# Batch 0's first 256 tokens alone through VectorE and ScalarE, with q and k loaded by kinds and layer one in tiles of four blocks

## The chip, the cores and the metric

The kernel runs on one core of a Trainium2 chip. The metric is the device time of one execution in microseconds (us); lower is better. PE is TensorE (DVE is VectorE, ACT is ScalarE, POOL is GpSimd, SP is SyncE), and "SPq" and "POOLq" are queues from which DMAs are issued.

## The reference, cut to what matters

Eight batches of eight heads, 576 tokens, head dimension 64. Heads 0 to 3 attend to the last 32 tokens ("plain"), heads 4 to 7 to every fourth of the last 128 tokens ("class": four residue classes of tokens, each a plain window of its own). The heads of a token are joined to a row of 512 values, and two dense layers follow.

```
scores = 0.125 * q @ k.T
plain   (heads 0-3): 0 <= rel < 32
dilated (heads 4-7): 0 <= rel < 128 and rel % 4 == 0
attn = softmax(where(mask, scores, -1e9));  x = attn @ v      # 4608 x 512
h = x @ w_in        # 512 x 2048
out = (h * sigmoid(h)) @ w_out     # 2048 x 512
```

## The kernel before, in words

The order of the work is written out by hand: under `tc.manual_schedule()` every engine executes its instructions in the order in which the Python code issues them, and the framework adds the semaphore waits. A batch passes through these steps (z = 0 is the plain kind, z = 1 the class kind):

- **Loads** (`load_qk`, `load_qk0`, `load_v`, `load_w_in`, `load_w_out`), all issued by POOL, with a cast from f32 to f16. POOL has eight semaphores for its DMAs and uses them in turn, so an issue waits until the DMA issued eight places earlier has landed. Two copies of `v` shifted by 32 tokens are made by small copies (`shift_plain`, `shift_class`, `shift_over`), for batch 0 partly on DVE and partly as DMAs from SP.
- **transpose** (L274; `transpose0` for batch 0, L301 class and L314 plain): PE turns q and k, DVE or ACT copy them out of PSUM into `kT`, `qT` (plain) and `kC`, `qC` (class).
- **scores** (L324 plain, L336 class): 32 x 64 products. For batch 0 the mask is laid into PSUM first by a product (`masks0`, L380) and the scores are added to it.
- **softmax**: the negative row maximum (`maxima0` L403, or L464), then either one subtraction on DVE (`shift0` L421) and one wide exponential on ACT (`exps` L487), or one narrow exponential for each slot with the maximum as bias and the sum read beside it (`exps` L496). `normal` then takes the sum (L505, only for the wide form), adds epsilon (L509), takes the reciprocal (L510) and multiplies (L512, the tile `pn`).
- **turn** and **turned**: PE transposes `pn` (L521) and DVE or ACT copy it out (L529, the tile `ptT`). **values0** (L580, L618) or **values** (L554, L618): the products with `v`; **finish0** (L593), **finish** (L631) and **last_finish** copy them into `xT`.
- **Layer one** (`layer1` L644; `layer1_part` L664 for batch 0): products with `w_in`, then silu on ACT into `gT` (L652, L671). **Layer two** (`layer2_first` L681 for batch 0, `layer2` L707): products with `w_out`, a copy (L691) and a store (L692).

Later batches run their attention inside the dense layers of the batch before: `plan_of(b)` keeps a list of steps, and `plan(s)` emits what is due at step s between two blocks of products. From batch 1 on the change moves only the transposes of batch 1 (in the steps of batch 0).

Batch 0 has nothing to hide behind. It is cut into part 0 (tokens 0 to 255) and part 1 (256 to 575). Before, the prologue runs part 0 and part 1 interleaved through the engines: the scores of part 1 follow those of part 0 on PE, and its maxima, shifts and exponentials stand on DVE and ACT between the steps of part 0. `keep_busy` (L841) fills waits of PE with products of the identity matrix. Then `layer1_part(f, part)` makes two of the 16 blocks of 128 features at a time, all 16 blocks for part 0 and then all for part 1; a tile `h` of two PSUM banks holds two blocks, and the pool `big` has two such tiles. In the steps -16 to -2 between the blocks of part 0 stand what is left of part 1's attention (`normal` and the steps after it), `clear_v(1)`, and the loads of v of batch 1, of w_out's last two quarters and of batch 2's q and k. The transposes of batch 1's class kind are at step 2, its scores at step 8, the transposes of its plain kind at step 17 and their scores at step 20 (steps 16 to 31 are in `layer2_first`, one for every four products).

The order of POOL's loads before: q and k of part 0 (two DMAs of all eight heads), q and k of part 1, v's first class group and plain heads, w_in's first quarter, v's second group and short rest, w_in's other quarters, batch 1's q and k (eight DMAs), w_out's first two quarters, batch 1's v.

Of the kernel before, what the change touches and what calls it, by code (L numbers as in the profile page):

```python
# [8 lines left out]
F16 = mybir.dt.float16  # L9
# [19 lines left out]
def kernel(  # L29
# [44 lines left out]
    ident_b = cpool.tile([P, P], BF16, name="ident_b")  # L74
    mask_b = cpool.tile([P, 2, 2, KB], BF16, name="mask_b")
    band_b = cpool.tile([P, KB], BF16, name="band_b")
# [18 lines left out]
    def load_qk(b):  # L95

        for which in (0, 1):
            t = nat.tile([P, H * 8, D], F16, tag=f"n{which}", name=f"n{which}_{b}")
            u0, u1 = 2 * URS[0], 2 * (URS[0] + URS[1])
            qk[b, 0, which] = t[:, 0:u0].rearrange("p (h u) d -> p h u d", h=2)  # L100
            qk[b, 1, which] = t[:, u0:u1].rearrange("p (h u) d -> p h u d", h=2)
        for z in (1, 0) if b == 1 else (0, 1):
# [8 lines left out]
    def load_qk0(part):  # L111

        t0, n = ((0, PA), (SA, PB))[part]
        qk0[part] = [None, None]
        for which, src in ((1, k), (0, q)):
            t = nat.tile([P, H * 8, D], F16, tag=f"n{which}", name=f"n{which}_0{part}")
            t = qk0[part][which] = t[:, 0 : H * UR].rearrange("p (h u) d -> p h u d", h=H)
            nc.gpsimd.dma_start(
                out=t[0:n],
                in_=src[0, :, t0 : t0 + n * UR].rearrange("h (p u) d -> p h (u d)", u=UR),  # L120
            )
# [77 lines left out]
    band = cpool.tile([P, KB], F32, name="band")  # L199
    nc.vector.memset(band[0:W], 0.0)  # L200
    clear_v(0, nc.vector)
    load_qk0(0)
# [10 lines left out]
    load_qk0(1)  # L213
    load_v(0, ("first", "plain"))
    shift_over(0, nc.sync.dma_start)
    shift_plain(0, nc.sync.dma_start, 4, NM)
    load_w_in(0, 1)
    load_v(0, ("second", "short"))
# [9 lines left out]
    for n in (1, 2, 3):  # L228
        nc.vector.tensor_copy(band[n * W : n * W + W], band[0:W])

    def lay_mask(m):
        n = 2 * m.shape[2]
        nc.vector.tensor_copy(
            m.rearrange("p a t c -> p (a t) c"), band[:, None, :].broadcast_to([P, n, KB])
        )
        nc.vector.memset(m[0:W, 0, 0, 0:W], NEG)
        nc.vector.memset(m[:, 1, 0, 0:W], NEG)

    lay_mask(mask_b)
    nc.vector.tensor_copy(ident_b, ident)  # L240
    nc.vector.tensor_copy(band_b, band)
# [699 lines left out]
```

## Time and profile before

| | us |
|---|---|
| median of 3 runs | 324.84 (324.49 to 325.32) |
| the profiled execution | 324.54 |
| its span, first to last instruction | 322.8 |
| outside the span | 1.7 |
| PE busy in the span | 311.8 |
| ACT, DVE, POOL busy | 214.7, 180.1, 83.2 |
| mean granted PE clock | 0.999 |

"Busy" counts the time in which at least one instruction of the engine is in flight. In a timeline line stand the start, the length of the whole merged group, engine, line, operation, output from input with sizes, the number of instructions, and in brackets how long the engine sat idle before it and for whom. In the chain of waits a line is one link of the chain that ended last. In a table of windows the number ahead of a bracket is the busy time of that engine in that stretch.

### The profile page before, as it was taken

The numbers are of one execution on the slowest core, as the hardware profiler recorded it, in microseconds if no ns is written. First come the engines' busy times: TensorE is split into PE (matmuls) and PEld (weight loads), VectorE is DVE, ScalarE is ACT, GpSimd is POOL, SyncE is SP. The second block draws the span as 40 slices with busy tenths as digits, with TensorE's granted clock in tenths as the row PEclk, the third lists the DMA queues.
The fourth block names the chain that finished last, engine by engine and source line by source line (L and its number), as shares of the span: only waits on it lengthen the run. The fifth ranks groups of instructions, "written<-read, shape, count | busy, mean of one in ns | idle before, by whom it ended". The sixth has DMA issues, their size and how long they took to land.

```text
span 322.8 us, 11769 instructions
## 1 busy us (share of the span) xinstructions
PE 311.8 (97%) x5151; PEld 202.0 (63%) x5151; DVE 180.1 (56%) x379; ACT 214.7 (67%) x700; POOL 83.2 (26%) x140
## 2 busy tenths in 40 slices
PE   5899999999999999999999999999999999999995
PEld 2667754677446775577645776567745776467544
DVE  5896679736597556663665446662576423620011
ACT  1776657657999569965896458975799357736300
POOL 8545537418404430335005700050000000000000
PEclk9999999999999999999999999999999999999999
DMA  8999999938924990298119840191011100110021
GB/s 108 187 212 198 184 230 204 227 99 124 184 86 83 129 146 36 73 163 133 26 68 140 170 80 2 67 174 37 5 52 49 65 4 0 68 67 0 2 97 67
DMA packets 45668, 32.63 MB, mean 101 GB/s; under 512 B 21264, under 2 KB 40336, under 8 KB 45616
## 3 DMA queue, kind: packets, MB, share of 16 engines
q0 software_dynamic: 39520, 21.73, 49.1%
q1 hardware_dynamic: 5952, 10.08, 8.5%
q8 instruction: 40, 0.66, 0.8%
q14 instruction: 12, 0.10, 0.1%
q10 hardware_dynamic: 144, 0.07, 0.1%
HBM read 37.75 MB, written 9.44 MB: 146 GB/s over the span
## 4 chain that ended last, share of the span: by engine, by line
PE 87%; DVE 6%; ACT 3%; issue 1%; POOL 1%; DMA 1%; POOLq 0%
PE h L644 35%; PE o L707 33%; PE h L664 4%; PE t L274 3%; PE x L554 3%; PE pt L521 2%; PE o L681 2%; PE s L336 2%; PE s L324 1%; DVE pn L512 1%; DVE ms L448 1%; ACT pe L496 1%; DVE nm L464 1%; PE x L580 1%; DVE ob L691 1%
## 5 line engine op out<-in xcount | busy, mean ns | idle before, releaser
L707 PE MATMUL o<-w_out,gT 128*128 128x512 f16 (+1 forms) x528 | 115.6, 373 | 0.0
L644 PE MATMUL h<-xT,w_in 128*128 128x288 f16 x896 | 115.4, 286 | 0.0
L652 ACT ACTIVATE gT<-h 128x576 f16<-128x576 f32 x112 | 72.8, 650 | 61.9 <-PE h L644 61.2
L644 PEld LDWEIGHTS <-w_in 128*128 128x128 f16 x896 | 85.7, 98 | 23.0 <-DVE xT L631 0.3
L496 ACT ACTIVATE pe<-ms,nm 128x64 f32<-128x64 f32 x246 | 81.6, 333 | 3.3 <-DVE nm L464 3.2
L707 PEld LDWEIGHTS <-gT 128*128 128x128 f16 x528 | 50.1, 98 | 53.0
L691 DVE COPY ob<-o 128x512 f32<-128x512 f32 (+1 forms) x36 | 24.6, 682 | 52.5 <-PE o L707 52.1
L496 ACT ACTIVATION_READ_ACCUMULATOR pe<-ms,nm 128x1 f32 x246 | 46.0, 187 | 0.0
L448 DVE SCALAR_TENSOR_TENSOR ms<-s,mask 128x512 f32<-128x512 f32 x28 | 19.2, 686 | 41.4 <-PE s L336 25.0
L127 POOL DMA_DIRECT2D vw<-in_v_dram x16 | 10.1, 640 | 76.9 <-PE x L554 75.5
L512 DVE TENSOR_TENSOR pn<-pe,r 128x640 f16<-128x640 f32 (+2 forms) x32 | 25.3, 792 | 1.1
L631 DVE CAST xT<-x 128x512 f16<-128x512 f32 x27 | 17.4, 686 | 12.0 <-PE xs L618 12.0
L464 DVE TENSOR_REDUCE nm<-ms 128x10 f32<-128x640 f32 (+1 forms) x28 | 22.0, 787 | 1.0
L106 POOL DMA_DIRECT2D n<-in_k_dram x28 | 16.5, 602 | 14.6 <-PE t L274 5.2
L106 POOL DMA_DIRECT2D n<-in_q_dram x28 | 16.4, 605 | 10.0 <-DMA w_out<-in_moe_w_out_dram 5.4
L664 PE MATMUL h<-xT,w_in 128*128 128x256 f16 (+1 forms) x128 | 17.9, 295 | 0.5 <-ACT gT L671 0.5
L529 DVE COPY ptT<-pt 128x640 f16<-128x640 f16 (+1 forms) x27 | 11.7, 468 | 8.0 <-PE pt L521 8.0
L664 PEld LDWEIGHTS <-w_in 128*128 128x128 f16 x128 | 12.5, 101 | 4.7 <-issue 1.2
L681 PE MATMUL o<-w_out,gT 128*128 128x512 f16 x64 | 15.1, 380 | 0.0
L671 ACT ACTIVATE gT<-h 128x512 f16<-128x512 f32 (+1 forms) x16 | 10.3, 650 | 7.1 <-PE h L664 6.9
L521 PE MATMUL pt<-ident,pn 128*128 128x128 f16 x152 | 12.4, 224 | 1.4 <-DVE pn L512 1.2
L521 PEld LDWEIGHTS <-pn 128*128 128x128 f16 x152 | 10.1, 99 | 4.7 <-DVE pn L512 1.5
(102 smaller groups left out, 267.6 us busy)
## 6 DMA issues: line engine op xcount, KB each, us to landing
out_dram<-ob SPq DMA_DIRECT2D x35, 256.0 KB, 2.1
n<-in_k_dram POOLq DMA_DIRECT2D x28, 144.0 KB, 5.4
n<-in_q_dram POOLq DMA_DIRECT2D x28, 144.0 KB, 5.5
vw<-in_v_dram POOLq DMA_DIRECT2D x8, 288.0 KB, 6.7
vw<-in_v_dram POOLq DMA_DIRECT2D x16, 128.0 KB, 4.8
w_in<-in_moe_w_in_dram POOLq DMA_DIRECT2D x4, 512.0 KB, 11.6
w_out<-in_moe_w_out_dram POOLq DMA_DIRECT2D x4, 512.0 KB, 10.6
vw<-vw POOLq DMA_DIRECT2D x12, 128.0 KB, 2.8
```

Of the source, the lines that this page charges most:

```text
L106: nc.gpsimd.dma_start(out=qk[b, z, which][i * HF : i * HF + UPS[z]].rearrange("p h u d -> p h (u d)"), in_=src[b, h : h + 2].rearrange("h ...
L448: nc.vector.scalar_tensor_tensor(out=ms[:, 0:8].rearrange("p (n t) c -> p n (t c)", n=2), in0=s[hi].rearrange("p n t c -> p n (t c)"), sca ...
L464: nc.vector.tensor_reduce(out=nm[:, 0:w], in_=ms[:, 0:w], axis=AX.X, op=ALU.max, negate=True)
L496: nc.scalar.activation(pe[:, t, :], slot(t), AF.Exp, scale=1.0 if b else scale, bias=nm[:, t : t + 1], accum_out=l[:, t : t + 1],)
L512: nc.vector.tensor_tensor(pn[:, 0:w], a["pe", z, hi][:, 0:w], r[:, 0:w, None].broadcast_to([P, w, KB]), ALU.mult)
L521: nc.tensor.transpose(t[:, i, :], a["pn", z, hi][:, 2 * i : 2 * i + 2].rearrange("p t c -> p (t c)"), ident)
L644: nc.tensor.matmul(h[:, half, 0:HS], w_in16[:, c, f * P : f * P + P], xT[:, c, half * HS : half * HS + HS], start=(c == 0), stop=(c == MC ...
L652: nc.scalar.activation(gT[:, f, s0 : s0 + S].rearrange("p (a c) -> p a c", a=2), h[:, :, 0:HS], AF.Silu)
L664: nc.tensor.matmul(h[:, i, 0 : c1 - c0], w_in16[:, c, (f + i) * P : (f + i + 1) * P], xT[:, c, c0:c1], start=(c == 0), stop=(c == MC - 1),)
L681: nc.tensor.matmul(o, gT[:, f, t * P : (t + 1) * P], w_out16[:, f, :], start=(f == 0), stop=(f == NFF - 1),)
L691: copy(ob, o)
L707: nc.tensor.matmul(o, gT[:, f, t * P : (t + 1) * P], w_out16[:, f, m0:m1], start=(f == 0), stop=(f == NFF - 1),)
```

## The change

- **q and k of batch 0 are loaded by kinds**: `load_qk0(part, z)` loads four heads at a time, class kind first. The tiles have a tag for each kind (`n10`, `n11`, `n00`, `n01`; two buffers each) in place of one for both.
- **Order of the loads**: part 0 class, part 0 plain, v first and plain, w_in's first quarter, part 1 class and plain, v second and short, w_in's other quarters, batch 1's class kind, w_out's first quarter, batch 1's plain kind, w_out's other quarters, then batch 1's v and batch 2's q and k. On SP `shift_over` moves behind `shift_plain`.
- **Masks of batch 0**: the stationary operand is `rep_b`, four identities of 32 side by side, with 32 rows of mask, in place of a 128-row identity; a short product (32 x 32 columns twice) adds the left edge of the plain kind. `lay_mask` (the f32 mask for the other batches) and `clear_v(1)` move to step 0 of batch 0.
- **Fillers**: eight products of a zero tile at the start (before: four of the identity), and 22 of 160 columns, then 3, 8, 5 and 1 of 128, between part 0's steps.
- **Prologue**: only part 0 runs through all its steps up to `xT`. Then part 1's class transposes and the first layer-one tile for part 0. `layer1_first(x)` makes four blocks in one tile of two banks and one silu for all four.
- **Part 1's attention stands between the four such tiles**: tile 0; scores, maxima and shifts of both kinds, both exponentials; tiles 1 and 2; `normal` and `turn` of the class kind, `normal` of the plain kind; tile 3; values of the class kind, `turn` and values of the plain kind, with batch 1's class transposes between. Its scores are in one-bank tiles of the pool `ps`, one for each half, and maxima and shifts are made half by half.
- **`layer1_rest`** then makes the 16 blocks for part 1, two at a time, as before. Batch 1's plain transposes move from step 17 to step 16.

The new order around layer one (the loads and the lines taken out of the old prologue are left out):

```diff
+    for which in (1, 0):
+        transpose0(0, 1, which, dve)
+    masks0(0, 0)
+    transpose0(0, 0, 1, act)
     scores0(1, 0)
     maxima0(1, 0)
     shift0(1, 0)
+    transpose0(0, 0, 0, act)
     exps(0, 1, 0)
+    scores0(0, 0)
     maxima0(0, 0)
     scaled0(0, 0)
     normal(0, 1, 0)
     exps(0, 0, 0)
+    shift_class(0, dve, 0, 1)
+    keep_busy(warm, 22, 160)
     turn(0, 1, 0)
+    turned(0, 1, 0)
+    keep_busy(warm, 3, 128)
+    values0(1, 0)
+    finish0(1, 0, (act, act))
     normal(0, 0, 0)
     shift_plain(0, dve, 0, 4)
+    keep_busy(warm, 8, 128)
     turn(0, 0, 0)
     turned(0, 0, 0, act)
+    keep_busy(warm, 5, 128)
     values0(0, 0)
     finish0(0, 0, both)
+    keep_busy(warm, 1, 128)
+    for which in (1, 0):
+        transpose0(1, 1, which, dve)
+    layer1_first(0, warm)()
+    for z in (1, 0):
+        if z == 0:
+            for which in (1, 0):
+                transpose0(1, 0, which, act)
+        masks0(z, 1)
+        scores0(z, 1)
+        maxima0(z, 1)
+        shift0(z, 1)
+    exps(0, 1, 1)
+    exps(0, 0, 1)
+    layer1_first(1)()
+    layer1_first(2)()
+    normal(0, 1, 1)
+    turn(0, 1, 1)
+    turned(0, 1, 1)
+    normal(0, 0, 1)
+    shift_class(0, dve, 1, 2)
+    layer1_first(3)()
+    values0(1, 1)
+    last_values(0, 1, (1,))
+    finish0(1, 1)
+    last_finish(0, 1, 1)
+    turn(0, 0, 1)
+    turned(0, 0, 1)
+    transpose(1, 1, 1, both)
+    values0(0, 1)
+    last_values(0, 0, (1,))
+    finish0(0, 1, both)
+    last_finish(0, 0, 1)
+    transpose(1, 1, 0, both)
...
-            for x in range(NFF):
-                plan(2 * x - NFF)
-                plan(2 * x + 1 - NFF)
-                layer1_part(2 * x % NFF, 2 * x // NFF, None if x else warm)
+            for f in range(0, NFF, 2):
+                plan(f)
+                plan(f + 1)
+                layer1_rest(f)
```

And the new functions for layer one:

```diff
+    def layer1_first(x, h=None):
+        if h is None:
+            h = big.tile([P, 2, 512], F32, tag="big", name=f"h_0_{x}_0")
+        h = h.rearrange("p a (i c) -> p a i c", c=SA)
+        for i in range(4):
+            for c in range(MC):
+                nc.tensor.matmul(
+                    h[:, i // 2, i % 2],
+                    w_in16[:, c, (4 * x + i) * P : (4 * x + i + 1) * P],
+                    state[0]["xT"][:, c, 0:SA],
+                    start=(c == 0),
+                    stop=(c == MC - 1),
+                )
+        return lambda: nc.scalar.activation(
+            gT[:, 4 * x : 4 * x + 4, 0:SA].rearrange("p (a i) c -> p a i c", a=2), h, AF.Silu
+        )
+
+    def layer1_rest(f):
...
+    def keep_busy(tile, n, m=512):
...
+            nc.tensor.matmul(tile[:, 0, 0:m], zeros[:, 0:P], zeros[:, 0:m], start=True, stop=True)
```

## The prediction

> **What bounds the kernel now.** I read the page first: PE is busy for nearly the whole span, DVE for about half.
>
> ```profile
> PE 311.8 (97%) x5151; PEld 202.0 (63%) x5151; DVE 180.1 (56%) x379; ACT 214.7 (67%) x700; POOL 83.2 (26%) x140
> ```
>
> The average hides the start, so next a table of windows, cut where batch 0 changes stage (up to the first layer-one product; layer one for part 0; for part 1; layer two; the rest). The first number after the window's length is PE's busy time, the third DVE's.
>
> ```profile
> 0.00:19.90 19.90, 14.89 (x336) 9.12 (x337) 15.14 (x46) 10.25 (x29) 13.44 (x26) 1.00 1.22 161
> 19.90:31.40 11.50, 10.79 (x171) 8.74 (x170) 9.10 (x22) 7.56 (x12) 4.83 (x8) 1.00 1.20 201
> 31.40:40.90 9.50, 9.50 (x188) 6.86 (x186) 5.71 (x10) 6.00 (x9) 5.24 (x8) 1.00 1.49 185
> 40.90:60.70 19.80, 18.85 (x381) 9.61 (x379) 17.15 (x35) 11.52 (x45) 10.99 (x19) 1.00 1.20 220
> 60.70:322.80 262.10, 257.81 (x4083) 167.63 (x4082) 132.98 (x269) 179.35 (x606) 48.70 (x81) 1.00 0.43 80
> ```
>
> From 31.4 on PE is full, but for batch 0's second layer (40.9 to 60.7), whose end waits for batch 1's softmax on DVE. The changed code ends ahead of that, so the result is the shift of one event: the start of layer two of batch 0, now 40.92. PE's timeline gives the pieces:
>
> ```profile
> 17.40 0.64 PE L580 MATMUL x<-ptT,vw 64*64 64x32 f16 x32
> ...
> 19.89 2.74 PE L664 MATMUL h<-xT,w_in 128*128 128x256 f16 x16
> 23.18 1.91 PE L664 MATMUL h<-xT,w_in 128*128 128x256 f16 x16 [0.55 <-ACT gT L671]
> ...
> 31.75 0.77 PE L274 MATMUL t<-ident,n 48*128 48x48 f16 x48
> 32.45 3.43 PE L664 MATMUL h<-xT,w_in 128*128 128x320 f16 x24
> 35.81 0.68 PE L336 MATMUL s<-kC,qC 64*32 64x64 f16 x64
> 36.31 0.32 PE L336 MATMUL ss<-kC,qC 64*32 64x64 f16 x16
> 36.56 4.52 PE L664 MATMUL h<-xT,w_in 128*128 128x320 f16 x32
> 40.92 1.03 PE L681 MATMUL o<-w_out,gT 128*128 128x512 f16 x4
> ```
>
> **Break-even.** From 32.45 to 40.92 lie 56 products of 320 columns and batch 1's class scores (36.56 - 35.81 = 0.75): (8.47 - 0.75) / 56 = 0.138 each. The new order has all 64, and the scores, behind batch 1's class transposes: 64 x 0.138 + 0.75 = 9.58. So the new kernel breaks even if the first product for part 1 (`layer1_rest`) starts at R = 40.92 - 9.58 = 31.3.
>
> **Part 0, to its xT (T0).** Durations are from DVE's and ACT's timelines; the chain of waits adds some 0.02 to a handover and 0.1 to 0.2 from PE's last product to its reader.
>
> Loads: the first 256 KB of k, issued at 1.26, landed 4.1 later (5.36), the next 256 KB 1.5 after that. Half a load so lands about 0.75 sooner: class k 4.6, class q 5.3. The plain k is still issued at 3.78 (behind POOL's ident and band) and lands 3.35 later at 7.1, the plain q at 7.85.
>
> - The eight zero products start with their memset (1.15) and take 0.427 each: 4.57. Masks 0.43, two groups of class transposes (0.54 each), copies on DVE (0.42): kC, qC ready at 6.65. The 32-row masks stream the same columns as before; they and the two small products end by 6.7 and are hidden by the wait for plain k. Without that cover they cost 0.1.
> - PE's next in line are the transposes of plain k, so the class scores queue behind its landing: 7.1 + 0.57 + 0.61 = 8.3 to DVE's maxima; 0.71 + 0.70: shifted at 9.7. Plain q's transposes, ACT's copy, plain scores: DVE's second maxima at 10.15, scaled at 11.05.
> - DVE: sum, epsilon, reciprocal, multiply 0.72 + 0.20 + 0.24 + 0.69 from 10.95: pn of the class kind at 12.8. ACT: eight narrow exponentials, 2.49, end at 13.55.
> - Turn 0.6 and copy 0.41: 13.9. Values 0.64, ACT's two copies 0.85: 15.4. DVE's plain pn 1.13 behind 13.95: 15.1; fillers to 15.4; turn 0.6, ACT's copy 0.58, values 0.64, copy 0.42: T0 = 17.7.
>
> These are products at half rate. In the lines above, 16 products of 256 columns took 2.74 at 19.89 and 1.91 at 23.18: the rate doubled at about 21.6, 4.2 after the start of an unbroken run at 17.40. The new fillers from 9.95 on (22 x 0.133 = 2.9) make such a run, so the rate should double by 14; from there turn, values and fillers take 0.2 to 0.4 less each: T0 = 17.0, which I take. Bounds: 16.0 (full rate from the first fillers; below) and 17.7, plus 0.85 if the first eight products of layer one are slow too (2.74 - 1.91).
>
> **From T0 to R.** Here the change costs. Before, part 1's maxima and shifts ran on DVE between part 0's steps; now they start only after layer one's first tile. DVE's rows for part 1:
>
> ```profile
> 13.72 0.96 DVE L403 TENSOR_REDUCE nm<-s 128x12 f32<-128x768 f32 x1 [0.21 <-PE s L336]
> 14.71 0.96 DVE L421 TENSOR_TENSOR ms<-s,nm 128x768 f32<-128x768 f32 x1
> ...
> 20.37 0.94 DVE L505 TENSOR_REDUCE l<-pe 128x12 f32<-128x768 f32 x1
> 21.35 0.33 DVE L509 TENSOR_SCALAR r<-l 128x12 f32<-128x12 f32 x1
> 21.71 0.23 DVE L510 RECIPROCAL r<-r 128x12 f32<-128x12 f32 x1
> 21.98 0.96 DVE L512 TENSOR_TENSOR pn<-pe,r 128x768 f16<-128x768 f32 x1
> 22.96 0.42 DVE L155 COPY vw<-vw 32x1024 f16<-32x1024 f16 x1
> ```
>
> - PE: tile 0, 16 x 0.109 = 1.75; masks 0.33; 48 scores 0.46; DVE begins at T0 + 2.75.
> - Class maxima and shifts in halves, about 0.46 each: + 4.6. ACT's silu table (1.28, beside tile 0), silu (about 1.0 for 1024 columns, from 0.60 for 512 and 0.70 for 640), kT and qT copies end at + 4.4; PE waits about 0.9 for them; plain scores + 4.85; plain maxima and shifts, four of 0.40: + 6.7. ACT's return to exp (1.28) hides under these: class exponential ends at + 6.5.
> - Class sum, epsilon, reciprocal, pn (0.98 + 0.36 + 0.27 + 0.96): + 9.25. Turn on PE, DVE idle 0.6, copy 0.55: + 10.4. Plain sum to pn 2.05, then the v copy (0.42), on which the class values wait: + 12.9. PE has ended tile 3 by + 11.5 (it waited for the silu of tile 1, behind both exponentials and a table load, until + 9.75) and stands until + 12.9.
> - Values and short values 0.45, x copies 0.67 and 0.28, the plain turn between; ptT 0.49: + 14.8. Batch 1's class transposes stand in that gap. Plain values 0.3, DVE's and ACT's halves of kC, x and xs copies: + 16.3.
>
> PE has 1.75 x 4 + 4.3 = 11.3 of work in these 16.3. So R = 17.0 + 16.3 = 33.3, 2.0 later than break-even. Batch 1's plain transposes a step earlier put DVE's copies off PE's path: about 0.2 back. **Sum: 40.92 + 2.0 - 0.2, or + 1.8**: 324.54 + 1.8 = 326.3 for a profiled execution. The runs' median is 0.3 above it, so I predict 326.6.
>
> **What I cost at nothing.** w_in's quarters: as many bytes lie ahead of the last three as before, so they land as before, at 20.8, 23.3 and 25.9 (issue plus landing); tiles 1, 2 and 3 want them at 21.9, 23.6 and 26.8. The first lies behind 640 KB less and lands near 12.8. If T0 is early the second one stops PE for under 1, but DVE, not PE, is late there. Batch 1's class kind lands by 29.7, wanted at 31.2. w_out's first quarter lands by 34, wanted at 42.9. Batch 1's v comes behind w_out, near 46, and SP's copies of it 6.5 later, 52.5, wanted at 57: if that is gone, PE stands in layer two. On POOL the issues only queue for each other; the new tags add no wait. clear_v(1) and lay_mask (1.9 + 1.5 on DVE) end 4.3 after R, and batch 1's class scores come at R + 5.1. shift_over behind shift_plain on SP has 15 us. The two added table loads (2.6) are on ACT ahead of waits that DVE ends.
>
> **Rivals.**
> - *Full rate from about 5.* The eight fillers, masks and transposes run from 1.15 to 6.6 with hardly a break, 5.4, more than the 4.2 after which the rate doubled before. Then transposes, scores, turns and values are short from the start: T0 = 16.0, R = 32.3: + 0.8, 325.6. Against it: products ran from 5.68 to 10.6 with few gaps before, and the 32 values at 17.40 were still slow. [...] The trace's granted clock reads 1.00 in all windows and shows no change.
> - *Half rate into layer one:* T0 = 17.7, and 0.85: + 3.3, 328.1. It needs the gaps between fillers to undo the run.
> - *Faster: the class kind feeds DVE early enough.* The price is the landing of plain k, on which everything in part 0 queues. The shortest landing of any POOL transfer in the trace is 2.2 (a 144 KB copy of v). With 2.2 in place of 3.35 and full rate from 5, T0 = 14.8, R = 31.1, and with the 0.2: - 0.4, 324.4 on the median's scale, no slower than before. It decides from a landing of about 2.6 after the issue. Against it: the first load found empty queues and took 4.1.
> - *The change does what it says, PE stays fed:* 11.3 from T0 = 16 would make R = 27.3 and the time 320.6. DVE's rows (some 13.6 between T0 + 2.75 and R) leave no room for it.
>
> **Chances.** Forecast 0.45; full rate early 0.25; half rate 0.12; early landing 0.12; PE fed 0.06. What a measurement of this kernel can tell from no change is about 0.3%, or 0.97, so 323.9 to 325.8 is "within". Faster: PE fed and a fifth of the early landing, 0.08. Within: the rest of that, and half of full rate early (its 325.6 is near the bound), with a little of the forecast's lower edge, 0.25. Slower: 0.67. The range goes from the early landing's time to a little over half rate's: 324.3 to 328.3.
>
> **What would show it.** T0: the first product of layer one after values of part 0, at 17.0 (before 19.9). R: the first product of 320 columns at 33.3. Between them DVE has hardly a gap and PE idles about 5, most of it ahead of the plain scores and of the class values, both released by DVE or ACT. Then layer two of batch 0 starts at 42.7 and lasts 19.6. I am wrong if PE is full between T0 and R, if the products wait for a DMA there, or if layer two of batch 0 gets shorter by over 0.5.

## The result, and the profile after

The changed kernel takes 332.35 us (median of 4 runs, 329.58 to 335.30); the kernel before, beside it, 324.95 (324.49 to 325.32). The ratio is 1.0151, 95% interval 1.0124 to 1.0177, so about 4.9 us more, where 1.8 were forecast. Two of the four runs (334.61 and 335.30) showed a granted clock of 0.97 to 0.98 and are left out of the ratio, which is why the median lies above it. The profiled execution took 330.08 with a span of 328.3 (before 324.54 and 322.8): its + 5.5 is what is taken apart here.

The changed kernel's page, the line of busy times:

```profile
PE 312.8 (95%) x5193; PEld 203.5 (62%) x5193; DVE 181.7 (55%) x385; ACT 215.4 (66%) x695; POOL 85.4 (26%) x144
```

PE does 1.0 more than before (311.8) and idles some 4.5 more. It also has 42 products and 42 weight loads more (5193 for 5151): 84 instructions, a number that comes back below.

Its table of windows, cut at the first product of layer one (17.13), the first for part 1 (R, 34.67), layer two of batch 0, layer one of batch 1, and the end. After the length: busy time of PE, PEld, DVE, ACT, POOL, then granted clock, DMA share and GB/s.

```profile
0.00:17.13 17.13, 13.04 (x254) 8.85 (x255) 11.29 (x36) 8.44 (x25) 12.09 (x25) 0.90 1.09 126
17.13:34.67 17.54, 13.36 (x340) 10.50 (x337) 12.33 (x28) 10.45 (x12) 9.01 (x15) 1.00 1.24 208
34.67:45.25 10.58, 10.58 (x223) 7.45 (x217) 8.48 (x20) 6.22 (x9) 4.66 (x8) 1.00 1.32 201
45.25:64.69 19.44, 17.90 (x312) 9.06 (x308) 16.52 (x34) 10.90 (x45) 10.91 (x18) 1.00 1.26 198
64.69:328.30 263.61, 257.92 (x4083) 167.60 (x4082) 133.03 (x269) 179.37 (x606) 48.73 (x81) 1.00 0.42 79
```

Between tile 0 and R PE is idle for 4.2 of 17.5. The last row holds the same 4083 products and as much busy time as before (257.92 and 257.81), yet lasts 263.61 in place of 262.10: 1.5 are lost in batches that the change does not touch.

PE's timeline shows the places:

```profile
15.99 0.46 PE L304 MATMUL t<-ident,n 80*128 80x80 f16 x8 [0.57 <-DMA n<-in_k_dram]
16.83 0.46 PE L304 MATMUL t<-ident,n 80*128 80x80 f16 x8 [0.38 <-DMA n<-in_q_dram]
17.13 1.91 PE L683 MATMUL h<-xT,w_in 128*128 128x256 f16 x16
...
23.08 1.92 PE L683 MATMUL h<-xT,w_in 128*128 128x256 f16 x16 [0.71 <-DMA w_in<-in_moe_w_in_dram]
25.63 1.92 PE L683 MATMUL h<-xT,w_in 128*128 128x256 f16 x16 [0.64 <-DMA w_in<-in_moe_w_in_dram]
27.39 0.50 PE L540 MATMUL pt<-ident,pn 128*128 128x128 f16 x6
28.49 1.92 PE L683 MATMUL h<-xT,w_in 128*128 128x256 f16 x16 [0.60 <-DMA w_in<-in_moe_w_in_dram]
31.22 0.44 PE L599 MATMUL x<-ptT,vw 64*64 64x32 f16 x32 [0.81 <-DVE vw L155]
...
49.67 0.28 PE L327 MATMUL s<-kT,qT 64*32 64x64 f16 x22 [0.37 <-issue]
...
123.20 0.53 PE L277 MATMUL t<-ident,n 64*64 64x64 f16 x42
124.77 0.44 PE L277 MATMUL t<-ident,n 64*64 64x64 f16 x30 [1.04 <-issue]
...
159.94 0.57 PE L277 MATMUL t<-ident,n 64*64 64x64 f16 x47
161.37 0.40 PE L277 MATMUL t<-ident,n 64*64 64x64 f16 x25 [0.87 <-issue]
```

Two kinds of wait are new. All three later tiles of layer one, and part 1's class q and k, wait for a DMA. And PE stands still for 0.4 to 1.0 in the middle of a run of short products of one line, with nothing that releases it ("issue").

The shift of PE's stages against before, from the two timelines:

| first product of | before | after | shift |
|---|---|---|---|
| layer one, batch 0 | 19.89 | 17.13 | - 2.77 |
| 320 columns (R) | break-even 31.3 | 34.67 | + 3.37 |
| layer one, batch 1 | 60.74 | 64.69 | + 3.95 |
| layer one, batch 2 | 102.41 | 106.22 | + 3.81 |
| layer two, batch 2 | 122.11 | 127.11 | + 5.00 |
| layer one, batch 3 | 138.99 | 143.98 | + 4.99 |
| layer two, batch 3 | 157.67 | 163.68 | + 6.01 |
| PE's last end | 318.97 | 324.98 | + 6.01 |

So + 3.9 is made in batch 0, and + 1.2 and + 1.0 at the two standstills near 124 and 161.

**Theories.** A: the loads come late (w_in and part 1's q and k), and DVE's chain from T0 to R does the rest. B: the standstills come from the borders between pieces of PE's program (the changed kernel's page has 40 packets on the queue named "instruction"). C: the clock granted to PE, once full, falls back to half in the waits (0.51 from 8.1 to 11.5; an open gate is in the recorded texts a granted clock of 1.0, a closed one 0.5). Rivals: D, the new order or its four-block tiles cost by themselves; E, the early zero products do harm.

### The profile page after: what moved, and what is told of

Same layout as the page of the kernel before. It is cut to its first block, busy times and chain, and to the rows that moved or that the text cites. A ratio compares the mean times of both kernels' runs of the same rounds, so it can differ in the third digit from the quotient of the medians.

```text
span 328.3 us, 11867 instructions
## 1 busy us (share of the span) xinstructions
PE 312.8 (95%) x5193; PEld 203.5 (62%) x5193; DVE 181.7 (55%) x385; ACT 215.4 (66%) x695; POOL 85.4 (26%) x144
## 4 chain that ended last, share of the span: by engine, by line
PE 83%; DVE 7%; DMA 6%; issue 2%; POOL 1%; ACT 0%
PE h L663 34%; PE o L743 32%; DMA w_in<-in_moe_w_in_dram 5%; PE t L277 3%; PE h L700 3%; PE x L573 3%; PE pt L540 2%; PE o L717 2%; DVE pn L531 1%; PE s L327 1%; PE s L339 1%; DVE ms L467 1%; DVE nm L483 1%; DVE l L524 1%; PE h L683 1%
## 5 line engine op out<-in xcount | busy, mean ns | idle before, releaser
L663 PEld LDWEIGHTS <-w_in 128*128 128x128 f16 x896 | 85.7, 98 | 23.0 <-DVE xT L650 0.3
L467 DVE SCALAR_TENSOR_TENSOR ms<-s,mask 128x512 f32<-128x512 f32 x28 | 19.2, 686 | 41.7 <-PE s L339 23.4
L650 DVE CAST xT<-x 128x512 f16<-128x512 f32 x27 | 17.4, 686 | 12.0 <-PE xs L637 12.0
L107 POOL DMA_DIRECT2D n<-in_q_dram x28 | 16.3, 601 | 9.4 <-DMA w_in<-in_moe_w_in_dram 2.5
L548 DVE COPY ptT<-pt 128x640 f16<-128x640 f16 (+2 forms) x29 | 12.7, 470 | 9.6 <-PE pt L540 9.6
L717 PE MATMUL o<-w_out,gT 128*128 128x512 f16 x64 | 14.8, 380 | 0.0
L277 PEld LDWEIGHTS <-n 64*64 64x64 f16 (+1 forms) x840 | 10.2, 101 | 6.5 <-issue 5.2
L277 PE MATMUL t<-ident,n 64*64 64x64 f16 (+1 forms) x840 | 12.3, 189 | 1.9 <-issue 1.9
L573 PEld LDWEIGHTS <-vw 64*64 64x64 f16 x896 | 8.4, 108 | 5.1 <-issue 5.0
```

The lines of the kernel that those rows point to most:

```text
L107: nc.gpsimd.dma_start(out=qk[b, z, which][i * HF : i * HF + UPS[z]].rearrange("p h u d -> p h (u d)"), in_=src[b, h : h + 2].rearrange("h ...
L277: nc.tensor.transpose(dst, w, ident[r, r])
L467: nc.vector.scalar_tensor_tensor(out=ms[:, 0:8].rearrange("p (n t) c -> p n (t c)", n=2), in0=s[hi].rearrange("p n t c -> p n (t c)"), sca ...
L663: nc.tensor.matmul(h[:, half, 0:HS], w_in16[:, c, f * P : f * P + P], xT[:, c, half * HS : half * HS + HS], start=(c == 0), stop=(c == MC ...
L717: nc.tensor.matmul(o, gT[:, f, t * P : (t + 1) * P], w_out16[:, f, :], start=(f == 0), stop=(f == NFF - 1),)
```

## The experiments

All ratios are to the kernel before, run on the same chip. The changed kernel's is 1.0151.

**phase_back**: theory B. PE's program is brought back to the place that it has before (84 + 172 = 256 instructions more, the estimated length of a piece).

```diff
+    def tiny(tile, n):
+        for _ in range(n):
+            nc.tensor.matmul(tile[0:W, 0, 0:2], zeros[0:W, 0:W], zeros[0:W, 0:2], start=True, stop=True)
...
-    layer1_first(1)()
-    layer1_first(2)()
+    tiny(h1, 28)
+    layer1_first(1, h1)()
+    tiny(h2, 29)
+    layer1_first(2, h2)()
```

(and 29 ahead of tile 3.)

> The changed kernel with 86 pairs of tiny zero products (32x32 weights, 2 columns) put into PE's waits ahead of layer one's tiles 1, 2 and 3, so that PE's program counts 172 instructions more there and 256 more than the kernel before from then on. Theory (PE's program comes in pieces of 256 instructions; the 84 instructions that the change adds moved the borders of these pieces into the runs of 72 transposes): the two gaps of about 1.0 among the transposes near 124 and 161, and the one of 0.4 among the scores near 49.7, are gone: span 328.3 - 2.2 = about 326. Rival (the gaps are waits for batches 3 and 4's q and k): they stay, span 328.3.

Ratio 1.0186 (1.0116 to 1.0255): no faster; the span is 330.1, not 326. The standstills near 124 and 161 are gone (layer two of batch 2 and of batch 3 are shifted by as much as layer one of batch 2, + 7.5), and so is the one near 49.7, so the rival, waits for q and k, falls. But one of 0.85 came at 48.43, in batch 1's plain transposes, which the change moved, and batch 0 was later: the granted clock is 0.5 from 7.6 to 14.4 and from 17.8 to 21.2, part 1's class k landed at 17.4 in place of 15.9, and R is 37.39. What B says of the place holds; the time was given back elsewhere.

**before_shifted**: B again, from the other side. The kernel before, with as many more instructions as the change adds.

```diff
     keep_busy(warm, 1)
+    for _ in range(42):
+        nc.tensor.matmul(warm[0:W, 0, 0:2], tz, tz[:, 0:2], start=True, stop=True)
```

> The kernel before with 42 products of 32 x 32 by 2 columns (84 instructions) in an early wait of PE, so that every later instruction stands at the same place in the program as in the changed kernel. Theory (PE's instructions come in pieces of 256 and a border that falls into a run of 72 short transposes costs about 1.0): two stalls of 0.8 to 1.1 with no releaser inside transposes of later batches appear near 120 and 157, and the time is 1.6 to 2.2 longer: 326.4 to 327.2. Rival (those stalls come from the order of the changed kernel, its loads or its later DVE work): no such stall, 324.5 to 325.4.

Ratio 1.0173 (1.0150 to 1.0196), 330.60: as slow as the changed kernel. PE's timeline:

```profile
19.74 0.29 PE L582 MATMUL x<-ptT,vw 64*64 64x32 f16 x8
22.18 0.51 PE L582 MATMUL x<-ptT,vw 64*64 64x32 f16 x24 [2.15 <-issue]
...
123.12 0.53 PE L276 MATMUL t<-ident,n 64*64 64x64 f16 x42
124.63 0.44 PE L276 MATMUL t<-ident,n 64*64 64x64 f16 x30 [0.98 <-issue]
```

The run of 72 transposes is cut into 42 and 30, at the same product as in the changed kernel; before it is whole. The one near 161 is there too (161.80, 1.44), and so is the one near 49.7 (0.39). That shows B for these: no load, wait or order of the change is needed for them, only 84 instructions ahead. The expected sum was too small, for one of 2.15 came ahead of layer one; the four make 5.0 of the span's + 6.4.

**before_shifted_early**: the same 42 products at the very start of PE.

```diff
+    for _ in range(42):
+        nc.tensor.matmul(busy[0:W, 0, 0:2], tz, tz[:, 0:2], start=True, stop=True)
     keep_busy(busy, 4)
```

> before_shifted with its 42 tiny products at the very start, where PE waits for the first load, and not between the values of part 0, where they themselves ran down a piece of the program just ahead of a border. Theory (the place of the borders alone costs): the stalls of 0.4 near 50, 1.0 near 123 and 1.0 to 1.5 near 160 are there again, the one of 2.15 ahead of layer one is gone or below 0.5: time 326.8 to 328.0. Rival (the tiny products cost as such, the borders little): 324.5 to 325.5. Second rival (the border ahead of layer one costs its 2 us wherever the tiny products stand): 329.5 to 331.

Ratio 1.0096 (1.0073 to 1.0119), 327.86, as the theory had it, though not all by its steps: the standstill ahead of layer one is 0.66, the one near 159 is 1.27, the ones near 50 and 123 are absent, and part 1's q landed 0.9 later. The later instructions stand at the same places in the program as in before_shifted, so the place alone does not decide: the border near 123 cost 1.0 there and nothing here, the one ahead of layer one 2.15 and 0.66. The timing around it must count too; what of it was not tested.

**dense_waits**: theory C. phase_back's 86 products are products of 128 x 128 by 128 columns, spread over nine waits.

```diff
+    keep_busy(busy, 14, 128)
     masks0(0, 0)
...
-    keep_busy(warm, 1, 128)
-    for which in (1, 0):
-        transpose0(1, 1, which, dve)
+    keep_busy(warm, 13, 128)
+    transpose0(1, 1, 1, dve)
+    keep_busy(warm, 8, 128)
+    transpose0(1, 1, 0, dve)
```

(and 8, 8, 8, 8, 14 and 6 ahead of part 1's plain masks, the tiles 1, 2 and 3, the class values and the plain values.)

> The changed kernel with 86 products of a zero tile (128 x 128 by 128 columns) in nine of PE's waits between 5 and 33 us, where phase_back had 86 tiny ones; nothing else differs from phase_back in the count of PE's instructions. Theory (the gate closes again after a 3.41 us window in which little of PE's array is used): from its first opening near 4.5 on no window is granted half rate, the granted clock is 0.993 or more in every run, the runs lie within 1.2 of each other, and the time is that of the changed kernel's best profiled execution without its two stalls of 1.0: 327.3 to 329.0. Rival (the spread of 328 to 336 comes from something else, late transfers above all): the spread and the granted clocks of 0.96 to 0.98 stay, median 330 to 333. Rival (the fillers themselves hold up the work): clock full, but first product for part 1 later than 35, time 330.

The clock held: granted 0.995 to 1.0 in all four runs (phase_back 0.98 to 0.99), and the runs lie within 2.4 (1.2 was expected; phase_back's lie within 4.4). The time did not follow: 330.86, ratio 1.0180 (1.0140 to 1.0221). The profile has full rate from 5.9 to the end, R at 35.51 (class q landed at 17.7, 0.9 later than in the changed kernel's profile), and standstills at other runs of short products:

```profile
46.53 0.41 PE L277 MATMUL t<-ident,n 64*64 64x64 f16 x28 [0.83 <-issue]
85.35 0.45 PE L277 MATMUL t<-ident,n 64*64 64x64 f16 x32 [0.65 <-issue]
```

So C holds in this profile: with the waits filled, the granted clock stays at 1.0 from 5.9 on. That full clock wins time is not shown. Full clock, R past 35 and a time of 330 are what the third case foresaw, in which the fillers themselves hold up the work; the later landing of class q may be as much to blame, and the two were not told apart.

**w_in_before_short**: theory A. v's short pieces are issued behind w_in.

```diff
-    load_v(0, ("second", "short"))
+    load_v(0, ("second",))
...
     load_w_in(3, 4)
+    load_v(0, ("short",))
```

> The changed kernel with the two short pieces of v issued after w_in's last quarter, so that w_in's second quarter waits for a load two places older. Theory (POOL's eight semaphores hold w_in's second quarter back until its first has landed at 15.1): it is issued by 13, the second, third and last quarter land up to 1 sooner (23.1, 25.6, 28.5 before), the first product for part 1 comes up to 1.0 sooner, span 327.3 to 328.0. Rival (the transfer rate of 200 KB a us sets the landings): they come sooner by the 96 KB that no longer stand ahead, 0.5, and not more.

w_in's last three quarters landed at 22.4, 24.8 and 27.6 (after: 23.0, 25.6, 28.4), only 0.6 to 0.8 sooner, though the second was issued at 10.5 in place of 15.4: nearer to the rival's 0.5 than to the theory's 1.0. Ratio 1.0193 (1.0128 to 1.0258): no faster, against an expected span of 327.3 to 328.0 (the profile has 331.8, R 35.93). The wait for a semaphore on POOL is a small part of the lag.

**wide_loads**: part 0's q and k of all heads in one DMA each, and part 1's too, as before the change, with the rest of the order kept.

```diff
-    load_qk0(0, 1)
+    load_qk0(0)
...
-    load_qk0(1, 1)
-    load_qk0(1, 0)
+    load_qk0(1)
```

> The changed kernel with q and k of each part of batch 0 loaded by one DMA each for all heads, as in the kernel before (part 0 first, part 1 behind w_in's first quarter); all else as changed. Theory (half-size loads at 0.63 each on POOL, with its four other instructions between them, starve the transfers from 3 to 13: 388 KB less by 13): part 0's chain starts about 0.9 later, but part 1's q and k land by 14.5 (16.0 and 16.8 before) and w_in's quarters about 2 sooner; layer one's first product at about 16.7 (17.1), the first product for part 1 at about 33 (34.7), span about 326.6. Rival (nothing is won, the landings follow the bytes alone): the late start of part 0 is added, span 329.

The rate came back (us 3 to 5: 68, 194, 198 GB/s, as before the change), but part 1's class q now lands with the plain one, at 20.4, and w_in at 24.1, 26.7 and 29.2, later than in the changed kernel and not 2 sooner, as the theory had it. Ratio 1.0277 (1.0203 to 1.0350): worse, and worse than the rival's span of 329, so undoing this part alone is no cure. Its profile has one thing to teach. Tile 0 starts so late that w_in is there for every tile, and no window from 24.7 to 38.4 is at half rate:

```profile
25.11 1.02 DVE L427 TENSOR_REDUCE nm<-s 128x6 f32<-128x384 f32 x2 [3.72 <-PE s L342]
```

From these first maxima for part 1 to R (38.86) are 13.75. The prediction's chain has 16.3 - 2.75 = 13.55 for it; the changed kernel took 34.67 - 19.99 = 14.68.

**one_quarter**: the tiles 1 to 3 read w_in's first quarter, so that they never wait for the others.

```diff
-                    w_in16[:, c, (4 * x + i) * P : (4 * x + i + 1) * P],
+                    w_in16[:, c, i * P : (i + 1) * P],
```

> The changed kernel with tiles 1 to 3 of layer one reading w_in's first quarter in place of theirs (12 of the 16 blocks of part 0 are computed with the wrong weights), so that none of them waits for a load. Theory (DVE's chain of part 1 is the bound, w_in only adds its last 1.1): the first product for part 1 comes about 16.4 after the first of layer one, at 33.5 in place of 34.7, span about 327.1. Rival (the landings of w_in bound the stretch): PE is fed, 11.3 after it, at 28.5, span about 322.

Ratio 1.0161 (1.0102 to 1.0221). The wait, 0.9 by the chains above, is 0.3%, less than this interval can show: inconclusive.

**no_early_open**: the eight zero products at the start cut to 8 columns.

```diff
-    keep_busy(big.tile([P, 2, 512], F32, tag="big", name="busy"), 8)
+    keep_busy(big.tile([P, 2, 512], F32, tag="big", name="busy"), 8, 8)
```

> The changed kernel with its eight zero products at the start cut to 8 columns each: every instruction stands where it stood, but nothing opens the gate at 4.6. Theory (the gate opens after a 3.41 us window with about three quarters of the array in use and closes after one with less than about a third): half rate at least until the 22 fillers have filled a window, 12 to 15; xT of part 0 ready 1 to 2 later than 15.75; the closings behind it as in the changed kernel; median 331 to 335. Rival (the early opening is what brings the closings, without it the gate opens once and stays): granted clock above 0.993 in all runs and a median of 329 to 330.5, better than the changed kernel's.

Ratio 1.0150 (1.0106 to 1.0195), that of the changed kernel; granted clocks 0.988 to 1.0, runs of 328.38 to 334.88. The early opening neither helps nor harms by an amount that shows here: the median, 330.80, lies between the theory's range and that of its rival. So rival E has nothing in its favour.

**before_early_gate**: the kernel before with eight such zero products and without the identity fillers.

```diff
-    keep_busy(big.tile([P, 2, 512], F32, tag="big", name="busy"), 4)
+    keep_busy(big.tile([P, 2, 512], F32, tag="big", name="busy"), 8)
...
-    keep_busy(warm, 1)
...
-    keep_busy(warm, 2)
...
-            nc.tensor.matmul(
-                tile[:, 0].rearrange("p (a c) -> p a c", c=P), ident,
-                ident[:, None, :].broadcast_to([P, 4, P]), start=True, stop=True,
-            )
+            nc.tensor.matmul(tile[:, 0], zeros[:, 0:P], zeros, start=True, stop=True)
```

> The kernel before with eight zero products of 512 columns as the first thing on PE, and without its later identity products. Theory (short products of 32 to 64 rows use too little of the array to hold the gate): full rate from about 5 for one window, then half rate again until layer one is dense, at 17 to 22; time 324.2 to 325.6, no gain. Rival (once open the gate stays open): full rate from 5 on, layer one for part 0 starts before 18.5, time 322.5 to 323.8, a version faster than both kernels.

Ratio 1.0004 (0.9983 to 1.0024; 10 runs): no gain. In its profile the clock was not full until about 23.5, not even for one window (the four masks of 256 columns at 5.68 take 1.04, for 1.03 in the kernel before, and 32 products of layer one 5.61 from 19.44), so the time is as the theory had it and the way to it is not.

**scores_first**: dense_waits, its fillers partly moved, with part 1's scores, maxima, shifts and exponentials of both kinds ahead of tile 0, w_in's first quarter behind part 1's q and k, the v copy in DVE's wait for the class turn, and `normal` of the plain kind behind the class values.

```diff
-    load_w_in(0, 1)
     load_qk0(1, 1)
     load_qk0(1, 0)
+    load_w_in(0, 1)
...
-    layer1_first(0, warm)()
...
     exps(0, 1, 1)
     exps(0, 0, 1)
+    layer1_first(0, warm)()
```

> dense_waits with the scores, maxima, shifts and exponentials of part 1's both kinds ahead of layer one's first tile (w_in's first quarter loaded behind part 1's q and k), the copy of v for the class values in DVE's wait for the class turn, and part 1's plain normal behind the class values. Theory (DVE's chain for part 1, begun only after tile 0, and the lag of the loads are what the change costs): DVE's maxima start by 18.5 in place of 20, the first product for part 1 comes at 30.5 to 32.0, the time is 323.3 to 325.3. Rival (w_in's lag of some 2 us holds the tiles whatever DVE does): PE waits for w_in ahead of the tiles 0, 2 or 3, first product for part 1 at 32.5 to 34, time 325.8 to 327.5.

Ratio 1.0211 (1.0169 to 1.0254). DVE's maxima start at 19.18, not by 18.5, and then stop 1.78 for PE, which stands still for 1.35 in the plain transposes at 20.86; the window that follows is at half rate. R is 36.95. The time, 331.08, is neither the theory's nor its rival's: the tiles did not wait for w_in, but stood behind PE's standstill, and the first ran at half rate (3.27 for 16 products, 1.91 for those of the next).

**scores_first_lean**: scores_first with part 1's class transposes and scores still earlier, and without the fillers that stood where the data was there.

```diff
-    keep_busy(warm, 5, 128)
+    for which in (1, 0):
+        transpose0(1, 1, which, dve)
     values0(0, 0)
     finish0(0, 0, both)
+    masks0(1, 1)
+    scores0(1, 1)
+    for which in (1, 0):
+        transpose0(1, 0, which, act)
```

> scores_first without the fillers that stood where the data was there: part 1's class transposes ahead of part 0's plain values, its class scores right behind them, its plain transposes next, no fillers in layer one; the eight zero products at the start are 94 of 48 columns, so that PE's instructions stand as in phase_back. Theory (order of DVE's chain, lag of w_in, gate and program borders are all that the change costs): DVE's first maxima for part 1 at 16.5 to 18, first product for part 1 (320 columns) at 31.3 to 33, PE held by w_in's quarters at 23, 25.5 and 28 alone, time 324.5 to 326.5 where no window is granted half rate after 10 us and up to 3 more where one or two are. Rival (the four-block tiles cost by themselves, by silu of 1024 columns and the two buffers): first product for part 1 at 34 or later with DVE early, time over 327.5.

Ratio 1.0081 (1.0063 to 1.0098), 327.65: about half of the changed kernel's loss is gone. The theory allowed up to 3 us for one or two windows at half rate, and the time lies within that. First maxima (19.0) and R (34.09) are both 1 later than the latest expected: the granted clock was at half from 8.6 to 15.4, and PE stood still once, ahead of tile 1, whose quarter of w_in had landed at 22.4:

```profile
24.16 1.91 PE L683 MATMUL h<-xT,w_in 128*128 128x256 f16 x16 [0.95 <-issue]
```

R and time are in the rival's range too (34 or later, over 327.5), but not by its condition: DVE was not early. From the first maxima to R are 15.1, 14.1 without the standstill, and wide_loads has 13.75 with the same tiles of four blocks, near the 13.55 of the prediction's rows. That speaks against a cost of the tiles themselves (D), but no version of the new order has tiles of two blocks, so it is argued and not shown. Behind batch 0 no time is lost: + 3.06 at layer two of batch 1, + 3.04 at the end.

**lean_dense**: scores_first_lean with the early fillers of dense_waits, its program shifted by 40 products to put the borders behind the runs that had stood still.

```diff
-    keep_busy(big.tile([P, 2, 512], F32, tag="big", name="busy"), 94, 48)
+    keep_busy(busy, 40, 112)
...
+    keep_busy(busy, 14, 128)
     masks0(0, 0)
```

> scores_first_lean with 14 zero products of 128 columns in the wait for plain k (as in dense_waits, where no window fell back to half rate) and 40 of 112 columns at the start in place of 94 of 48, so that the borders of the program fall 40 products later: past the end of the runs of short products in which the changed kernel and phase_back stood still. Theory (gate, borders and the order of DVE's chain are what the change costs, and what is left is w_in's landing at 22.5, 25 and 27.7): clock full from about 5 on, DVE's first maxima for part 1 at 17 to 18, first product for part 1 at 31.5 to 33, time 324.2 to 326.0, level with the kernel before. Rival (the borders only move to other short runs): full clock, but stalls with no releaser of 1 or more in sum, time 326.3 to 328.

Ratio 1.0163 (1.0130 to 1.0196), 330.09: later than either case had it. The rival was right in its cause, the borders fell into other runs, but not in its full clock. PE's timeline, and a table of windows (the number before the last two is the granted clock):

```profile
17.22 0.33 PE L317 MATMUL t<-ident,n 80*64 80x80 f16 x8
19.23 1.01 PE L317 MATMUL t<-ident,n 80*64 80x80 f16 x24 [1.68 <-issue]
```

```profile
14.10:17.50 3.40, 2.91 (x111) 2.22 (x111) 2.77 (x7) 1.10 (x3) 1.95 (x3) 1.00 1.23 211
17.50:24.30 6.80, 5.12 (x87) 3.58 (x83) 4.03 (x9) 2.46 (x4) 3.04 (x5) 0.50 1.27 208
```

The standstill alone is 1.68, from 17.55 to 19.23. It did not bring the half clock: the clock falls to half at 17.51, just ahead of it, behind a window in which PE was busy for 2.91 of 3.40, mostly with short products. The standstill lies in the first of the two windows at half rate, and tile 0 begins in the second, at 22.05.

No version beats the kernel before; before_early_gate equals it.

## Why the prediction was wrong

The direction was right, and so was part of the reason (DVE's chain behind T0). The size was not: + 5.5 in the profiled execution for + 1.8. Two steps failed, both costed at nothing: the landing of the loads in batch 0, and the rest of the program "as before". Where the 3.7 come from (T0 is the end of the last copy into part 0's xT):

| step of the prediction | forecast | measured | difference |
|---|---|---|---|
| T0 | 17.0 | 15.75 | - 1.25 |
| T0 to DVE's first maxima for part 1 | 2.75 | 4.24 | + 1.49 |
| those to R | 13.55 | 14.68 | + 1.13 |
| R to layer one of batch 1 (31.3 to 60.74 before, less 0.2) | 29.24 | 30.02 | + 0.78 |
| from there to PE's end | as before | 2.06 more | + 2.06 |
| behind PE's end | as before | 3.32 for 3.83 | - 0.51 |

- **T0.** 17.0 rested on half rate until 14. The rival "full rate from about 5" was near on T0 (16.0): the granted clock went to full at 4.6. That is partly luck, for plain k landed 0.5 sooner than assumed, and what none of the cases had worked against it: the clock fell back to half from 8.1 to 11.5. Three windows of the changed kernel, with the granted clock as the number ahead of the last two:

```profile
4.60:8.10 3.50, 2.90 (x87) 1.93 (x86) 1.39 (x3) 0.89 (x2) 3.50 (x6) 0.99 0.98 113
8.10:11.50 3.40, 2.97 (x52) 2.81 (x53) 3.15 (x8) 2.35 (x12) 3.05 (x5) 0.51 1.64 126
11.50:14.90 3.40, 2.48 (x70) 2.08 (x70) 2.79 (x8) 2.27 (x11) 0.56 (x1) 1.00 1.28 188
```

  PE is busy for 2.9 of the first 3.5, mostly with masks, transposes and scores of 32 and 64 rows; the next 3.4 run at half. The prediction's view of the clock (1.00 in all windows of before) could not have shown it: the first granted-clock record of before lies at 21.6, and the view reads 1.00 ahead of it too, though layer one's products of 256 columns start 0.213 apart up to there and 0.109 behind it; from there the record holds 1.00 up to 322. The sign named for T0, the first product of layer one at 17.0, came at 17.13, and that is luck too: xT was ready at 15.75, and PE then waited for part 1's class k and q.
- **"w_in's quarters: as many bytes lie ahead of the last three as before, so they land as before"** is the step that failed in batch 0. They landed at 23.0, 25.6 and 28.4 in place of 20.8, 23.4 and 25.9. The bytes are as many, but the queue was hungry at the start. What the DMAs moved in each us from 0 to 40, the changed kernel and then the kernel before:

```profile
GB/s 0 0 22 155 88 111 166 106 129 157 85 151 192 193 191 191 198 224 246 197 206 206 208 202 220 199 206 208 207 203 203 208 205 202 218 196 202 210 202 208
```

```profile
GB/s 0 0 15 68 197 197 189 193 161 188 172 159 190 216 197 208 214 208 224 232 198 206 210 204 208 217 198 200 207 199 180 179 199 196 165 186 195 188 166 169
```

  Over us 2 to 13 that is 1362 KB for 1729, and from there both run at some 200 KB per us: 367 / 200 = 1.8 that is not made up. By the same rows 3.39 MB had been moved when the second quarter landed before and 3.43 MB after, so the lag is one of bytes. That larger first transfers would take it away is not shown: wide_loads had them, and there the second quarter landed behind 3.9 MB, which this account does not explain. Before, POOL's first four issues carry 256 + 256 + 320 + 320 KB and are out by 4.5; now they carry four times 128 KB and are out by 4.25. w_in's first quarter, costed as landing near 12.8, landed at 15.1, and the q and k of part 1 behind it at 15.95 and 16.79, later than T0, which was not thought of. Hence + 1.49 ahead of the maxima (PE's rows at 15.99 and 16.83, then tile 0 ahead of the scores), and most of + 1.13 behind them: DVE idles 1.49 ahead of the class ptT where 0.6 was foreseen, as the turn stands behind tile 2 and its wait for w_in.

```profile
19.99 1.02 DVE L424 TENSOR_REDUCE nm<-s 128x6 f32<-128x384 f32 x2 [2.17 <-PE s L339]
27.93 0.56 DVE L548 COPY ptT<-pt 128x768 f16<-128x768 f16 x1 [1.49 <-PE pt L540]
```

  So the sign "DVE has hardly a gap" did not come: DVE is busy for 12.33 of the 17.54 between tile 0 and R. wide_loads, where w_in was there, has 13.75 for the forecast's 13.55: behind the maxima the chain itself was sized right. The sentence "if T0 is early the second one stops PE for under 1, but DVE, not PE, is late there" missed that the turn, on which DVE waits, is queued on PE behind it.
- **The other rivals.** Half rate into layer one and "PE stays fed" did not come (16 products of tile 0 took 1.91; PE idles 4.2 of 17.5). Plain k landed 2.9 behind its issue (6.56 for 7.1), between the forecast's 3.35 and the 2.6 from which that rival decides. The prediction named "the products wait for a DMA there" as a sign of being wrong; it was one.
- **The 0.2 won by batch 1's transposes a step earlier** is not seen. The stage from R to layer one of batch 1 took 0.78 more than forecast, 0.37 of it the standstill at 49.67.
- **The rest of the program "as before"** cost 2.06, more than the 1.8 of the whole forecast. This term was not in the sum at all, and before_shifted shows it to be one of the place of PE's instructions. On the queue named "instruction" the changed kernel's page has 40 packets and 0.66 MB, 16 KB each, beside 10,386 of PE's instructions (5193 products with their weight loads), 260 to a packet; phase_back, with 172 more, has 5 packets in its first 40 us where the changed kernel has 4. The standstills lie at products 862, 2269 and 2909 of the changed kernel's trace, which is 94 or 93 more than a multiple of 128, and the two long ones end about 1.5 behind the landing of a packet (123.26 and 124.77; 159.80 and 161.37). In all 14 profiles, each of the 28 standstills above 0.3 with no releaser lies 93 to 95 behind such a multiple; the kernel before has none. A packet of about 256 instructions, 128 products with their weight loads, is the author's estimate from these counts and places. Most of the 40 borders cost nothing that shows; those that show lie mostly in runs of short products, at 0.3 to 2.7 each (2.72 at 163.27 of no_early_open). That PE stands still because it waits for the next packet is inferred from these places and times; no view names the wait.

The clock, in one view. I cut the first 48 us or so of twelve profiles (before, after and the experiments but for one_quarter and no_early_open) along the edges of their granted-clock records, which lie 3.41 apart or a multiple of it (4.64, 8.05 and 11.46 in the changed kernel), and worked out for each window an estimate, the used share: rows / 128 times columns / 128 times output columns of every product (128 x 128 is the largest here), over the output columns that fit into the window. For half rate that is 512 in 0.427, as the eight zero products of the changed kernel start 0.427 apart, and twice as many for full (0.216 apart in layer two). Ahead of a profile's first record the rate is taken as half, as before's products have it.

| next window | windows | used share |
|---|---|---|
| half, then full | 23 | 0.73 and more |
| half, stays half | 30 | 0.75 and less |
| full, then half | 11 | 0.35 and less |
| full, stays full | 107 | 0.32 and more |

In the changed kernel the windows from 1.22 and 8.05, followed by full rate, used 0.88 and 0.84, and the one from 4.64, followed by half, 0.19; in before the one from 14.8, followed by half, used 0.67 and the one from 18.2, followed by full, 0.81. The rows overlap narrowly, and what sets the clock is not shown beyond these windows. PE's busy share does not divide them so: full windows behind which the clock fell were busy for 39% to 86% (2.91 of 3.40 in lean_dense, from 14.1), those behind which it stayed full for 58% and more (1.97 of 3.40 there, from 10.7). Behind these 48 us none of the twelve falls back before PE's work ends (the changed kernel's record of 1.00 runs from 11.46 to 328.9). And dense_waits, which added 128 x 128 products and nothing else, is the one version of the new order in whose profile it never fell (1.0 from 5.9 on). In the window from 4.64 of the changed kernel, followed by half rate, PE had no gap longer than 0.68. The used share also fits before_early_gate, where the clock did not rise early: its window from 3.0 used 0.69.

**What stays open.** Why one border is hidden and the next costs 2 was not settled; the place in the program and the traffic on the DMA queues both differ between the kernels. So the share of the 4.9 that belongs to the order, rather than to where the borders happened to fall, is known only roughly: the changed kernel's own profile puts 2.6 of its 5.5 on standstills (0.37 + 1.19 + 1.02), and no kernel of the new order was run without any (the nearest are phase_back, with one of 0.85 and three windows at half rate, and scores_first_lean, with one of 0.95). What is left, some 3, is put down to the loads and DVE's chain by the waits in one profile; no experiment took these away and won the time back. And the loads vary: with the same order of loads w_in's second quarter landed at 23.0 (the changed kernel), 23.9 (dense_waits) and 24.4 (phase_back).

## What to carry to other kernels

Here the sum of bytes ahead of a transfer did not say when it would land: smaller first transfers behind the same spacing of issues went with a hungry queue at the start (1362 KB for 1729 over us 2 to 13) and a lag of 1.8 that was not made up. So check the first microseconds of the transfer rate and what the queued consumer stands in front of. PE is full in this kernel, and 84 more PE instructions, which move the borders of its program, cost the kernel before as much as the whole change (42 idle products and their weight loads 3.1 or 5.6 by the ratios, by where they stood, for the change's 4.9); shift the program by a few dozen harmless products in both versions before a difference of 1 or 2% is put down to the order. Read the clock of each window of some 3.4, not the mean: here the clock fell to half behind windows of waits and short products with a used share of 0.35 or less, and the next stage paid.

## What the runs showed of the hardware

- From 4.6 to 8.1 of the changed kernel PE was busy for 83% of the time with small products (an estimated used share of 0.2), and the granted clock of the next window was 0.51; in the first 48 us of the twelve profiles every window at full rate that was followed by half rate had used 0.35 or less.
- The queue "instruction" moved 40 packets of 16 KB beside 10,386 of PE's instructions. The standstills with no releaser, 93 to 95 products behind a multiple of 128, took 0.3 to 2.7 each, and the same place cost 0.98 in before_shifted and nothing in before_shifted_early (near 123); 84 instructions added at the start of the kernel before cost 3.1, and ahead of part 0's plain values 5.6.
- A standstill of 1.35 lay in a window with an estimated used share of 0.26, and the next window ran at half rate (scores_first, 18.9 to 22.3 and on to 25.7; 16 products there took 3.27).
